# Value tiles of one bank and late mirror products in the first block of an FFT and gated-FFN kernel, with one shared stage-1 table

## The chip, the cores and the metric

One of the eight cores of a Trainium2 chip (trn2). The first rounds of experiments ran on chip 7, those that start with after_again on chip 0 and the last three on chip 7 again, each time with the kernel before in the same rounds. The metric is the device time in microseconds (us) of one execution, as the median of several. The profile gives a second figure, the span from the first to the last instruction, which is 1.7 to 2.1 us shorter; each timed execution lists it. "Product" alone means an elementwise product on VectorE (DVE); ScalarE is ACT, TensorE PE, GpSimd POOL.

## The reference, cut to what matters

```python
def _attn_ref(x):                       # x: (8, 3008, 256), fp32
    X = np.fft.fft(x, axis=1)
    X = np.fft.fft(X, axis=2)
    return X.real.astype(np.float32)

def _moe_ref(x, w_gate, w_val, w_out):  # x: (24064, 256), d_ff 1536
    gate = np.maximum(x @ w_gate, 0.0)
    val = x @ w_val
    return (gate * val @ w_out).astype(np.float32)
```

The kernel does the long transform in two stages (94 times 32 points), folds the transform over 256 into the weights, and uses the mirror symmetry of a real input's transform: from one set of matmuls it gets the gate and value of a frequency ("direct") and, after one more matmul that adds in place, those of the mirrored frequency. A batch has three blocks of 512 columns; a block has 12 steps f (t counts steps over all blocks). The first block (t from 0 to 11) is the only one in which DVE makes both products; later, POOL makes the mirror product and steps go in pairs.

## The kernel before

The value tile of a first-block step takes two banks of PSUM and uses one; there are two such tiles. The mirror matmul (`k == 2`) adds into the bank that the direct product reads.

```python
    psv = ctx.enter_context(tc.tile_pool(name="psv", bufs=2, space=PS))
    # ...
    def early(name):                       # PSUM tiles of the start: value and output tiles in turn
        turn["v"] += 1
        return psv.tile([128, 2, 512], F32, tag="v", name=name)[:, 0, :] if turn["v"] % 2 else spare(name)
    # ...
    def gate(t):                           # two matmuls into a gate bank (of two), then Relu on ACT
        # ...
        nc.scalar.activation(pair(t, "gs")[:, t % 2, ds], G[:, ds], ACTF.Relu)

    def mirror_gate(t):                    # adds into the same bank, after that Relu has read it
        # ...
    # ... the first block:
    for t in range(NF + 1):
        if t:
            mirror_gate(t - 1)
        if t < NF:
            gate(t)
        if t:
            value(t - 1, 2)
            mirror_h(t - 1, 1, nc.vector, pair(t - 1, "V"))
        if t < NF:
            value(t, 0)
            value(t, 1)
            direct_h(t, 1)
            between(t)                     # weight folding, stage 2 of the next blocks: t = 0 to 8 only
```

In the start, the first gate weights arrive by DMA, DVE makes their sum and their difference, and the first fold takes both:

```python
    def pair_w(n, i, eng, parts=(0, 1)):
        lo, hi, up = (wst[i, n, c] for c in range(3))
        if 0 in parts:
            eng.tensor_tensor(up, lo, hi, op=ALU.add)
        if 1 in parts:
            eng.tensor_tensor(lo, lo, hi, op=ALU.subtract)

    def fold_w(n, i, cs, ps=None):
        ps = ps or spare("psw")
        for k, w in ((0, wst[i, n, 2]), (1, wst[i, n, 0])):          # the sum, the difference
            nc.tensor.matmul(ps[64 * k:64 * k + 64, :], lhsT=cd[:, cs, 64 * k:64 * k + 64], rhs=w,
                             start=True, stop=True)
        # ... evictions
```

`cd` is the D table, the cosines and sines with which the fold multiplies the weights: three activations on ACT. The stage-1 table `wn` lives in a pool that closes after the start, so ACT copies half of it to `w1` for the later batches.

Of the kernel before, what the change touches and what calls it, by code (L numbers as in the profile page):

```python
# [11 lines left out]
F32 = mybir.dt.float32  # L12
BF16 = mybir.dt.bfloat16
I32 = mybir.dt.int32
ALU = mybir.AluOpType
ACTF = mybir.ActivationFunctionType
SB = bass.MemoryType.SB
PS = bass.MemoryType.PSUM
# [26 lines left out]
def kernel(ctx: ExitStack, tc, x, w_gate, w_val, w_out, out):  # L45
# [3 lines left out]
    nc = tc.nc  # L49
    B, S, D = x.shape  # L50
    DF = w_gate.shape[1]
    NA, NB = 94, 32
    H = D // 2
    NF = DF // 128
# [7 lines left out]
    tp = ctx.enter_context(tc.tile_pool(name="tp", bufs=2, space=SB))  # L62
    hp = ctx.enter_context(tc.tile_pool(name="hp", bufs=HB, space=SB))
    psg = ctx.enter_context(tc.tile_pool(name="psg", bufs=2, space=PS))
    psv = ctx.enter_context(tc.tile_pool(name="psv", bufs=2, space=PS))
    pso = ctx.enter_context(tc.tile_pool(name="pso", bufs=1, space=PS))
    pqp = ctx.enter_context(tc.tile_pool(name="pqp", bufs=5, space=SB))

    ctx.enter_context(tc.manual_schedule())

# [64 lines left out]
                in_offset=bass.IndirectOffsetOnAxis(ap=ixf[:, k:k + 1], axis=0))  # L135

    turn = {"o": 0, "v": 0}

    def spare(name):

        turn["o"] += 1
        return pso.tile([128, 512], F32, tag=f"o{turn['o'] % 2}", name=name)
# [5 lines left out]
    def early(name):  # L148

        turn["v"] += 1  # L150
        return psv.tile([128, 2, 512], F32, tag="v", name=name)[:, 0, :] if turn["v"] % 2 else spare(name)

    t1t = {}

    def stage1(b, c, evac):

        ps, eo = borrow("ps1"), xt[b]["eo"]
        for i in range(2):
            jj = 2 * c + i
            o = ps[0:96, i * D:(i + 1) * D]  # L160
            if jj:
                nc.tensor.matmul(o, lhsT=w1[:, jj, :], rhs=eo[:, jj, :], start=True, stop=True)  # L162
                continue
            for cs, lo, hi in ((0, 0, H + 1), (1, H + 1, D)):
                for k in range(2):
                    nc.tensor.matmul(ps[0:96, lo:hi], lhsT=wz[:, cs, k, :], rhs=eo[:, k * (J - 1), lo:hi],  # L166
                                     start=(k == 0), stop=(k == 1))
        evacuate(b, c, ps, evac)
# [9 lines left out]
        else:  # L178
            nc.vector.tensor_copy(dst, src)

    psf, tabs = {}, {}

    def ends(r, n):

# [99 lines left out]


    ix = const.tile([96, 2, B], I32, tag="ix")
    w1 = const.tile([NA, 16, 96], BF16, tag="w1")
    wz = const.tile([NA, 3, 2, 96], BF16, tag="wz")
    m2 = const.tile([128, 2, 128], BF16, tag="m2")
    rot = const.tile([128, 128], BF16, tag="rot")  # L290
# [57 lines left out]
    with tc.tile_pool(name="sp", bufs=1, space=SB) as sp:  # L348
        dve, pl = nc.vector, nc.gpsimd

        def residue(t, q, n, eng):

            eng.tensor_scalar(q, t, scalar1=1.0 / n, scalar2=RND, op0=ALU.mult, op1=ALU.add)
            eng.tensor_scalar(q, q, scalar1=-RND, scalar2=float(n), op0=ALU.add, op1=ALU.mult)
            eng.tensor_tensor(t, t, q, op=ALU.subtract)

        def sines(out, r, n, sign):
            nc.scalar.activation(out, r, ACTF.Sin, scale=sign * 2.0 * math.pi / n * (1.0 - 2e-7))

        def cosines(out, a, n):  # L360

            nc.scalar.activation(out, a, ACTF.Sin, scale=-2.0 * math.pi / n, bias=qpi[0:a.shape[0], :])

        def absolute(out, a):
            nc.scalar.activation(out, a, ACTF.Abs)
# [1 line left out]
        def iota(eng, out, pattern, base, mult):  # L367
            eng.iota(out, pattern=pattern, base=base, channel_multiplier=mult, allow_small_or_imprecise_dtypes=True)

        wn = tabs["wn"] = sp.tile([NA, 2, 16, 96], BF16, tag="wn", name="wn")  # L370
        tabs["wzn"] = sp.tile([NA, 2, 96], BF16, tag="wzn", name="wzn")
        tabs["back"] = sp.tile([NA, NB, H], BF16, tag="back", name="back")
        ixf = sp.tile([96, 3], I32, tag="ixf")
# [60 lines left out]
        def bits(shift, mask):  # L434
            ti = sp.tile([128, 1], I32, tag=f"b{shift}{mask}i")
            dve.tensor_scalar(ti[:], pi[:], scalar1=shift, scalar2=mask,
                              op0=ALU.logical_shift_right, op1=ALU.bitwise_and)
            tf = sp.tile([128, 1], F32, tag=f"b{shift}{mask}f")
            dve.tensor_copy(tf[:], ti[:])
            return tf  # L440
# [23 lines left out]
        for k in range(2):  # L464
            sines(free(wz[:], 192 * (k + 1), [97, 2], [2, 48]), both[0], S, 2.0 * k - 1.0)
        nc.scalar.mul(wn[:, 0, 9:16, :], wn[:, 1, 9:16, :], -1.0)
        nc.scalar.copy(w1[:, 1:10, :], wn[:, 1, 1:10, :])
        back(0, 2, "dve")
        dve.tensor_scalar(da[:], dd[:], scalar1=mi[:], scalar2=None, op0=ALU.mult)
        residue(da[:], dq[:], D, dve)  # L470
        jj, sl, up, odd = bits(0, 15), bits(4, 1), bits(5, 3), bits(0, 1)

        ends(24, 8)
# [34 lines left out]
        ends(16, 4)  # L508
        back(16, 4, "dve")
        dve.tensor_scalar(tis[:], tis[:], scalar1=NB - 1, scalar2=None, op0=ALU.bitwise_and)  # L510
        absolute(dq[:], da[:])
        cosines(cd[:, 0, 1:H], dq[:, 1:H], D)
        sines(cd[:, 1, 1:H], da[:, 1:H], D, 1.0)
        group((6, 7, 0), False)
        first_evac(4, "act")
        nc.sync.dma_start(out=seen[:], in_=t1t[0][0:1, 0, 8:10])
# [10 lines left out]
        first_evac(0, "dve")  # L527
        for cs in range(2):
            dve.tensor_tensor(m2[:, cs, :].rearrange("p (u k) -> p u k", u=4), sv[cs][:], ui[:], op=ALU.mult)
        nc.scalar.copy(w1[:, 10:16, :], wn[:, 1, 10:16, :])  # L530

        iota(pl, di[:], [[-32, 4], [-16, 2], [-1, 16]], 0, 1)
        pl.tensor_scalar(s2[:], mi[:], scalar1=1.0, scalar2=-2.0, op0=ALU.min, op1=ALU.mult)
# [43 lines left out]
    op = ctx.enter_context(tc.tile_pool(name="op", bufs=2, space=SB))  # L577

    steps = [(b, blk, f) for b in range(B) for blk in range(NBLK) for f in range(NF)]
    pairs = {}  # L580

    LO, HI = NB // 2, 512 - NB // 2

# [5 lines left out]
    def direct(t):  # L589

        blk = steps[t][1]
        return slice(LO if blk == 0 else 0, HI + 1 if blk == NBLK - 1 else 512)

    def split(t):

        return t >= NF

    def pair(t, name):

        e = pairs.setdefault(t // 2, {})  # L600
        if name == "V" and not split(t):
            name = f"V{t % 2}"
            if name not in e:
                e[name] = psv.tile([128, 2, 512], F32, tag="v", name="V")
            return e[name]
        if name not in e:
            pool, shape, dt = {"h": (hp, [128, 2, 2, 512], BF16), "gs": (gp, [128, 2, 512], F32),
                               "V": (psv, [128, 2, 512], F32), "gm": (ep, [128, 2, 512], F32),
                               "E": (ep, [128, 2, 512], F32)}[name]
            e[name] = pool.tile(shape, dt, tag=name.lower(), name=name)  # L610
        return e[name]
# [3 lines left out]
    def gate(t):  # L615
        b, blk, f = steps[t]
        pq, fs, ds = pqt[b, blk], slice(f * 128, (f + 1) * 128), direct(t)
        G = Gt[t] = psg.tile([128, 512], F32, tag="g", name="G")
        nc.tensor.matmul(G[:, ds], lhsT=wc[0][:, fs], rhs=pq[:, 0, ds], start=True, stop=False)  # L619
        nc.tensor.matmul(G[:, ds], lhsT=ws[0][:, fs], rhs=pq[:, 1, ds], start=False, stop=True)  # L620
        nc.scalar.activation(pair(t, "gs")[:, t % 2, ds], G[:, ds], ACTF.Relu)  # L621
# [8 lines left out]
    def value(t, k):  # L630
        b, blk, f = steps[t]
        cs = mirrored(t) if k == 2 else direct(t)
        w = (wc, ws, wm)[k][1]
        nc.tensor.matmul(pair(t, "V")[:, t % 2, cs], lhsT=w[:, f * 128:(f + 1) * 128],  # L634
                         rhs=pqt[b, blk][:, min(k, 1), cs], start=(k == 0), stop=(k > 0 or split(t)),
                         skip_group_check=(k == 2 or k == 1 and split(t)))

# [6 lines left out]
    def direct_h(t, n):  # L644

        ds, k = direct(t), slice(t % 2, t % 2 + n)
        nc.vector.tensor_tensor(pair(t, "h")[:, k, 0, 0:ds.stop - ds.start], pair(t, "gs")[:, k, ds],  # L647
                                pair(t, "V")[:, k, ds], op=ALU.mult)

    def mirror_h(t, n, eng, val):  # L650

        cols, k = mirrored(t), slice(t % 2, t % 2 + n)
        w = cols.stop - cols.start
        eng.tensor_tensor(free(pair(t, "h")[:], 1024 * (t % 2) + 512 + w - 1, [1024, n], [-1, w]),  # L654
                          pair(t, "gm")[:, k, cols], val[:, k, cols], op=ALU.mult)

    def mirror_value(p):
        t = 2 * p
# [126 lines left out]
    def between(t):  # L785
        for fn in extra.get(t, ()):
            fn()
        pace(t)

    for t in range(NF + 1):  # L790
        if t:
            mirror_gate(t - 1)
        if t < NF:
            gate(t)
        if t:
            value(t - 1, 2)
            mirror_h(t - 1, 1, nc.vector, pair(t - 1, "V"))
        if t < NF:
            value(t, 0)
            value(t, 1)  # L800
            direct_h(t, 1)
            between(t)

    for p in range(NF // 2, n + NF // 2):
        t = 2 * p
        live = p < n
        if NF // 2 < p <= n:
            mirror_gate(t - 1)
        if live:
            value(t, 0)  # L810
            value(t + 1, 0)
            gate(t)
        out_piece(t - NF, 0)
        between(t)
        if NF // 2 < p <= n:
            direct_h(t - 2, 2)
        if live:
            even(t)
            even(t + 1)
        out_piece(t - NF, 1)  # L820
        if live:
            mirror_gate(t)
            gate(t + 1)
        out_piece(t + 1 - NF, 0)
        between(t + 1)
        if NF // 2 < p <= n:
            mirror_value(p - 1)
        if live:
            value(t, 1)
            value(t + 1, 1)  # L830
        out_piece(t + 1 - NF, 1)
# [30 lines left out]
```

## Time and profile before

| | before |
|---|---|
| time, median of the first 3 runs | 624.94 us (624.94 to 625.77) |
| span of the profiled run | 623.9 us |
| PE busy | 612.0 us, 98% of the span |
| start of DVE's sum of the first gate weights | 15.21 us |
| first gate matmul of step 0 | 21.99 us |
| first output matmul (step 12) | 51.81 us |

The prediction below shows the lines of the page and of the views. A row has the start, the duration, engine and source line, operation, what is written from what, shapes, a count of merged rows, and in brackets the idle time before and what ended it.

```profile
15.21 0.69 DVE L321 TENSOR_TENSOR wst<-wst 128x512 f32<-128x512 f32 x1 [0.53 <-DMA wst<-in_moe_w_gate_dram]
15.94 0.69 DVE L323 TENSOR_TENSOR wst<-wst 128x512 f32<-128x512 f32 x1
16.62 1.13 PE L333 MATMUL psw<-wst,cd 128*64 128x512 f32 x4
```

DVE waits for the weights, makes the sum (15.21) and the difference (15.94, ready at 16.63).

### The profile page before, as it was taken

How to read it: one execution, taken by the hardware profiler on the slowest of the kernel's cores; microseconds unless marked ns; L12 is line 12 of the kernel's file. 1: busy time of each engine (PE TensorE's matmuls, PEld its weight loads, DVE VectorE, ACT ScalarE, POOL GpSimd, SP SyncE). 2: the span in 40 equal slices, each digit the busy share in tenths (PEclk: the TensorE clock that was granted, in tenths of full speed). 3: DMA queues.
4: the chain of work that ended last, by engine and by line, in shares of the span. 5: the costliest groups of instructions: out<-in, count | busy, mean ns of one | idle time of the engine just before them, and what ended most of it. 6: DMA issues, size and time to landing. Idle time of an engine off the chain costs nothing.

```text
span 623.9 us, 11929 instructions
## 1 busy us (share of the span) xinstructions
PE 612.0 (98%) x4252; PEld 409.3 (66%) x4284; DVE 536.7 (86%) x652; ACT 445.5 (71%) x857; POOL 520.0 (83%) x447
## 2 busy tenths in 40 slices
PE   8999999999999999999999999999999999999996
PEld 4345666766666666666667666666666666666665
DVE  7677898899889898888988998898988888899991
ACT  7676777777776767767677767767677776766660
POOL 8898898999888898899988998888988965565664
PEclk9999999999999999999999999999999999999998
DMA  8994282525553182613833255531822134112114
GB/s 168 240 169 109 82 219 67 134 65 163 125 136 79 34 234 71 164 36 86 222 100 92 63 162 127 134 82 34 230 72 61 34 85 125 52 34 67 34 35 99
DMA packets 42038, 67.44 MB, mean 108 GB/s; under 512 B 5877, under 2 KB 31774, under 8 KB 39962
## 3 DMA queue, kind: packets, MB, share of 16 engines
q1 hardware_dynamic: 37162, 50.61, 31.4%
q0 software_dynamic: 4656, 15.88, 10.7%
q8 instruction: 33, 0.54, 0.4%
q10 hardware_dynamic: 160, 0.20, 0.1%
q14 instruction: 27, 0.22, 0.1%
HBM read 38.85 MB, written 30.17 MB: 111 GB/s over the span
## 4 chain that ended last, share of the span: by engine, by line
PE 96%; DMA 1%; POOL 1%; issue 1%; DVE 1%; ACT 0%; POOLq 0%; DVEq 0%
PE po L683 40%; PE V L634 19%; PE G L619 10%; PE G L626 10%; PE G L620 10%; PE psw L333 2%; PE ps L162 2%; PE ps L271 2%; DMA lo<-in_x_dram 1%; POOL hi L132 0%; DVE h L647 0%; PE pst L240 0%; PE ps L216 0%; PE ps L166 0%; POOL lo L129 0%
## 5 line engine op out<-in xcount | busy, mean ns | idle before, releaser
L654 POOL TENSOR_TENSOR h<-gm,E 128x992 bf16<-128x992 f32 (+1 forms) x138 | 319.9, 2318 | 83.3 <-DVE E L661 54.4
L683 PE MATMUL po<-wo,h 128*128 128x256 bf16 (+2 forms) x2304 | 328.5, 272 | 0.4
L683 PEld LDWEIGHTS <-h 128*128 128x128 bf16 (+2 forms) x2304 | 231.4, 103 | 105.9
L628 ACT ACTIVATE gm<-G 128x496 f32<-128x496 f32 (+1 forms) x288 | 170.4, 592 | 94.7 <-PE G L626 87.7
L647 DVE TENSOR_TENSOR h<-gs,V 128x1024 bf16<-128x1024 f32 (+3 forms) x150 | 173.8, 1159 | 59.4 <-PE V L634 39.3
L641 DVE SCALAR_TENSOR_TENSOR E<-nb,af,V 128x496 f32<-128x496 bf16 (+1 forms) x276 | 190.2, 731 | 0.4 <-PE G L620 0.4
L621 ACT ACTIVATE gs<-G 128x497 f32<-128x497 f32 (+2 forms) x288 | 169.7, 589 | 25.3 <-PE G L620 25.2
L661 DVE SCALAR_TENSOR_TENSOR E<-E,V 128x992 f32<-128x992 f32 (+1 forms) x138 | 164.6, 1193 | 0.0
L619 PE MATMUL G<-pq,wc 128*128 128x496 bf16 (+2 forms) x287 | 107.6, 375 | 1.2
L620 PE MATMUL G<-pq,ws 128*128 128x497 bf16 (+2 forms) x288 | 108.0, 375 | 0.1
L626 PE MATMUL G<-pq,wm 128*128 128x496 bf16 (+1 forms) x288 | 107.9, 375 | 0.0
L634 PE MATMUL V<-pq,ws 128*128 128x496 bf16 (+2 forms) x280 | 83.7, 374 | 0.0
L634 PE MATMUL V<-pq,wc 128*128 128x496 bf16 (+2 forms) x266 | 80.7, 374 | 0.0
L620 PEld LDWEIGHTS <-ws 128*128 128x128 bf16 x288 | 28.2, 98 | 32.6
L696 ACT COPY os<-po 128x512 f32<-128x512 f32 x63 | 36.9, 586 | 14.3 <-PE po L683 11.7
L634 PEld LDWEIGHTS <-wc 128*128 128x128 bf16 x288 | 28.2, 98 | 20.7 <-issue 2.5
L114 POOL TENSOR_TENSOR eo<-xla 94x256 bf16<-94x256 f32 x56 | 40.5, 729 | 0.6
L619 PEld LDWEIGHTS <-wc 128*128 128x128 bf16 x288 | 28.2, 98 | 18.5 <-DVE pq L278 0.8
L114 POOL TENSOR_TENSOR eo<-xlb 94x256 bf16<-94x256 f32 (+1 forms) x42 | 34.4, 820 | 0.7
L111 POOL TENSOR_TENSOR xla<-xla,xha 94x510 f32<-94x510 f32 x28 | 32.9, 1175 | 2.2
L177 ACT CAST t<-ps 96x512 bf16<-96x512 f32 x56 | 32.7, 584 | 2.3 <-PE ps L162 0.2
L626 PEld LDWEIGHTS <-wm 128*128 128x128 bf16 x288 | 28.1, 98 | 4.4 <-issue 1.6
(142 smaller groups left out, 367.8 us busy)
## 6 DMA issues: line engine op xcount, KB each, us to landing
out_dram<-os SPq DMA_DIRECT2D x124, 128.0 KB
Td<-t SPq DMA_DIRECT2D x7, 768.0 KB
t<-Td SPq DMA_DIRECT2D x7, 768.0 KB
out_dram<-os SPq DMA_DIRECT2D x82, 64.0 KB
xla<-in_x_dram SPq DMA_DIRECT2D x7, 720.0 KB
xlb<-in_x_dram SPq DMA_DIRECT2D x6, 640.0 KB
nb<-Nd SPq DMA_DIRECT2D x23, 128.0 KB
out_dram<-os SPq DMA_DIRECT2D x40, 48.0 KB
```

The source lines that it names most:

```text
L114: yield eng.tensor_tensor(e1[:, :, k:k + H], x1[:, :, 0:H], free(x1, D, [DX, n], [-1, H]), op=op)
L619: nc.tensor.matmul(G[:, ds], lhsT=wc[0][:, fs], rhs=pq[:, 0, ds], start=True, stop=False)
L620: nc.tensor.matmul(G[:, ds], lhsT=ws[0][:, fs], rhs=pq[:, 1, ds], start=False, stop=True)
L621: nc.scalar.activation(pair(t, "gs")[:, t % 2, ds], G[:, ds], ACTF.Relu)
L626: nc.tensor.matmul(G[:, cols], lhsT=wm[0][:, f * 128:(f + 1) * 128], rhs=pqt[b, blk][:, 1, cols], start=False, stop=True, skip_group_check ...
L628: nc.scalar.activation(pair(t, "gm")[:, t % 2, cols], G[:, cols], ACTF.Relu)
L634: nc.tensor.matmul(pair(t, "V")[:, t % 2, cs], lhsT=w[:, f * 128:(f + 1) * 128], rhs=pqt[b, blk][:, min(k, 1), cs], start=(k == 0), stop=( ...
L641: nc.vector.scalar_tensor_tensor(pair(t, "E")[:, t % 2, cols], nbt[b, blk][:, cols], af[:, f:f + 1], pair(t, "V")[:, t % 2, cols], op0=ALU ...
L647: nc.vector.tensor_tensor(pair(t, "h")[:, k, 0, 0:ds.stop - ds.start], pair(t, "gs")[:, k, ds], pair(t, "V")[:, k, ds], op=ALU.mult)
L654: eng.tensor_tensor(free(pair(t, "h")[:], 1024 * (t % 2) + 512 + w - 1, [1024, n], [-1, w]), pair(t, "gm")[:, k, cols], val[:, k, cols], o ...
L661: nc.vector.scalar_tensor_tensor(E[:, :, cols], E[:, :, cols], 2.0, V[:, :, cols], op0=ALU.mult, op1=ALU.subtract)
L683: nc.tensor.matmul(po[0:m, i, :], lhsT=pair(t - f + ff, "h")[:, ff % 2, sg, g * 128:g * 128 + m], rhs=wo[:, ff, :], start=(ff == 0), stop= ...
```

## The change

Its intent: give each value of the first block its own bank, so that the mirror matmul and the mirror product can come one step late, after the direct product of the next step; give the start four tiles where it had two; move the D table ahead on ACT; keep the table `wn` for the whole run and drop the copy, paying for its room with one of the five buffers of pq, the transformed block that the gate and value matmuls read.

```diff
-    psv = ctx.enter_context(tc.tile_pool(name="psv", bufs=2, space=PS))
     pso = ctx.enter_context(tc.tile_pool(name="pso", bufs=1, space=PS))
-    pqp = ctx.enter_context(tc.tile_pool(name="pqp", bufs=5, space=SB))
+    singles = ctx.enter_context(ExitStack())
+    ps1 = singles.enter_context(tc.tile_pool(name="psf", bufs=4, space=PS))
+    pqp = ctx.enter_context(tc.tile_pool(name="pqp", bufs=4, space=SB))
...
-        return psv.tile([128, 2, 512], F32, tag="v", name=name)[:, 0, :] if turn["v"] % 2 else spare(name)
+        return ps1.tile([128, 512], F32, tag="v", name=name) if turn["v"] % 2 else spare(name)
...
-                nc.tensor.matmul(o, lhsT=w1[:, jj, :], rhs=eo[:, jj, :], start=True, stop=True)
+                nc.tensor.matmul(o, lhsT=wn[:, 1, jj, :], rhs=eo[:, jj, :], start=True, stop=True)
...
-        nc.scalar.copy(w1[:, 1:10, :], wn[:, 1, 1:10, :])
...
         residue(da[:], dq[:], D, dve)
+        absolute(dq[:], da[:])
+        cosines(cd[:, 0, 1:H], dq[:, 1:H], D)
+        sines(cd[:, 1, 1:H], da[:, 1:H], D, 1.0)
... (these three lines stood after the eighth input part; a second copy to w1 goes too)
-    for t in range(NF + 1):
+    for t in range(NF):
         if t:
             mirror_gate(t - 1)
-        if t < NF:
-            gate(t)
+        gate(t)
+        value(t, 0)
+        value(t, 1)
+        direct_h(t, 1)
         if t:
-            value(t - 1, 2)
-            mirror_h(t - 1, 1, nc.vector, pair(t - 1, "V"))
... 
+            last_value(t - 1)
+        between(t)
...
+        if p == NF // 2:
+            gate(t)
+            last_value(t - 1)
+            singles.close()
+            psv = ctx.enter_context(tc.tile_pool(name="psv", bufs=2, space=PS))
```

The last lines are the hand-over at step 12: the pool of four small tiles is closed and its banks go to the two-bank tiles of the later blocks.

More of the change, by code (lines that the diff above doesn't have):

```diff
@@ L137 @@
     turn = {"o": 0, "v": 0}
+    tabs = {}
     def spare(name):
@@ L179, in evacuate @@
             nc.vector.tensor_copy(dst, src)
-    psf, tabs = {}, {}
+    psf = {}
     def ends(r, n):
@@ L286 @@
     ix = const.tile([96, 2, B], I32, tag="ix")
-    w1 = const.tile([NA, 16, 96], BF16, tag="w1")
+    wn = tabs["wn"] = const.tile([NA, 2, 16, 96], BF16, tag="wn", name="wn")
     wz = const.tile([NA, 3, 2, 96], BF16, tag="wz")
@@ L368, in iota @@
             eng.iota(out, pattern=pattern, base=base, channel_multiplier=mult, allow_small_or_imprecise_dtypes=True)
-        wn = tabs["wn"] = sp.tile([NA, 2, 16, 96], BF16, tag="wn", name="wn")
         tabs["wzn"] = sp.tile([NA, 2, 96], BF16, tag="wzn", name="wzn")
@@ L510 @@
         dve.tensor_scalar(tis[:], tis[:], scalar1=NB - 1, scalar2=None, op0=ALU.bitwise_and)
-        absolute(dq[:], da[:])
-        cosines(cd[:, 0, 1:H], dq[:, 1:H], D)
-        sines(cd[:, 1, 1:H], da[:, 1:H], D, 1.0)
         group((6, 7, 0), False)
@@ L529 @@
             dve.tensor_tensor(m2[:, cs, :].rearrange("p (u k) -> p u k", u=4), sv[cs][:], ui[:], op=ALU.mult)
-        nc.scalar.copy(w1[:, 10:16, :], wn[:, 1, 10:16, :])
         iota(pl, di[:], [[-32, 4], [-16, 2], [-1, 16]], 0, 1)
@@ L579 @@
     steps = [(b, blk, f) for b in range(B) for blk in range(NBLK) for f in range(NF)]
-    pairs = {}
+    pairs, singly, psv = {}, {}, None
     LO, HI = NB // 2, 512 - NB // 2
@@ L596, in split, with single @@
         return t >= NF
+    def single(t):
+        if t not in singly:
+            singly[t] = ps1.tile([128, 512], F32, tag="v", name="V")
+        return singly[t].unsqueeze(1)
     def pair(t, name):
         e = pairs.setdefault(t // 2, {})
-        if name == "V" and not split(t):
-            name = f"V{t % 2}"
-            if name not in e:
-                e[name] = psv.tile([128, 2, 512], F32, tag="v", name="V")
-            return e[name]
         if name not in e:
@@ L633, in value @@
         w = (wc, ws, wm)[k][1]
-        nc.tensor.matmul(pair(t, "V")[:, t % 2, cs], lhsT=w[:, f * 128:(f + 1) * 128],
+        o = pair(t, "V")[:, t % 2, cs] if split(t) else single(t)[:, 0, cs]
+        nc.tensor.matmul(o, lhsT=w[:, f * 128:(f + 1) * 128],
                          rhs=pqt[b, blk][:, min(k, 1), cs], start=(k == 0), stop=(k > 0 or split(t)),
@@ L646, in direct_h @@
         ds, k = direct(t), slice(t % 2, t % 2 + n)
+        val = pair(t, "V")[:, k, ds] if split(t) else single(t)[:, :, ds]
         nc.vector.tensor_tensor(pair(t, "h")[:, k, 0, 0:ds.stop - ds.start], pair(t, "gs")[:, k, ds],
-                                pair(t, "V")[:, k, ds], op=ALU.mult)
+                                val, op=ALU.mult)
     def mirror_h(t, n, eng, val):
@@ L654, in mirror_h @@
         eng.tensor_tensor(free(pair(t, "h")[:], 1024 * (t % 2) + 512 + w - 1, [1024, n], [-1, w]),
-                          pair(t, "gm")[:, k, cols], val[:, k, cols], op=ALU.mult)
+                          pair(t, "gm")[:, k, cols], val[:, :, cols], op=ALU.mult)
     def mirror_value(p):
@@ L788, in between, with last_value @@
         pace(t)
-    for t in range(NF + 1):
+    def last_value(t):
+        value(t, 2)
+        mirror_h(t, 1, nc.vector, single(t))
+    for t in range(NF):
         if t:
             mirror_gate(t - 1)
-        if t < NF:
-            gate(t)
+        gate(t)
+        value(t, 0)
+        value(t, 1)
+        direct_h(t, 1)
         if t:
-            value(t - 1, 2)
-            mirror_h(t - 1, 1, nc.vector, pair(t - 1, "V"))
-        if t < NF:
-            value(t, 0)
-            value(t, 1)
-            direct_h(t, 1)
-            between(t)
+            last_value(t - 1)
+        between(t)
     for p in range(NF // 2, n + NF // 2):
@@ L806 @@
         live = p < n
-        if NF // 2 < p <= n:
+        if p <= n:
             mirror_gate(t - 1)
+        if p == NF // 2:
[3 more added lines that the diff above has]
+            psv = ctx.enter_context(tc.tile_pool(name="psv", bufs=2, space=PS))
         if live:
@@ L811 @@
             value(t + 1, 0)
-            gate(t)
+            if p > NF // 2:
+                gate(t)
         out_piece(t - NF, 0)
```

## The prediction

> **What bounds the kernel now.** I read the page first (busy shares), then the busy time of each engine in seven stretches, then PE's waits over the whole span, then the order in time where PE is not full.
>
> ```profile
> PE 612.0 (98%) x4252; PEld 409.3 (66%) x4284; DVE 536.7 (86%) x652; ACT 445.5 (71%) x857; POOL 520.0 (83%) x447
> ...
> PE 96%; DMA 1%; POOL 1%; issue 1%; DVE 1%; ACT 0%; POOLq 0%; DVEq 0%
> ```
>
> PE is busy in 98% of the span, and 96% of the chain that ended last is PE. So only holes in PE are worth time. The busy time by stretches (length, then PE, PEld, DVE, ACT, POOL) says where the holes are:
>
> ```profile
> 0.00:16.60 16.60, 13.84 (x92) 8.24 (x93) 12.83 (x54) 12.45 (x28) 12.79 (x34) 1.00 0.76 158
> 16.60:22.00 5.40, 5.40 (x36) 1.79 (x35) 3.77 (x9) 3.92 (x8) 5.16 (x6) 1.00 0.84 255
> 22.00:45.00 23.00, 22.80 (x136) 8.76 (x135) 16.00 (x26) 16.31 (x33) 21.68 (x26) 1.00 1.02 213
> 45.00:51.80 6.80, 5.35 (x23) 2.12 (x22) 4.76 (x9) 3.77 (x8) 6.41 (x12) 1.00 0.51 108
> 51.80:100.00 48.20, 48.04 (x344) 33.14 (x346) 41.34 (x47) 36.72 (x70) 42.17 (x38) 1.00 0.48 126
> 100.00:560.00 460.00, 458.74 (x3222) 314.23 (x3244) 410.36 (x456) 338.83 (x649) 394.79 (x313) 1.00 0.40 105
> ```
>
> After 51.8 us PE is full. Holes are in the first 16.6 us (tables and first input) and from 45.0 to 51.8, the last four f steps of the first block, where no weight folding is left to fill PE. PE's waits over the whole span, all before 52 us:
>
> ```profile
> PE V L634 <- DVE h L647: 1.4, 3, 0.8
> PE psk L398 <- DVE wk L392: 1.3, 1, 1.3
> PE ps L216 <- DVE hi L190: 0.9, 1, 0.9
> PE ps L216 <- ACT t L230: 0.4, 1, 0.4
> PE psw L333 <- DVE wm L327: 0.2, 1, 0.2
> ```
>
> The change can touch the first and the fourth. The first in order of time (step 10 and the hand-over to step 12; G is the gate, V the value, wm the mirror weights):
>
> ```profile
> 48.22 0.37 PE L620 MATMUL G<-pq,ws 128*128 128x496 bf16 x1
> 48.24 0.66 DVE L647 TENSOR_TENSOR h<-gs,V 128x496 bf16<-128x496 f32 x1
> 48.69 0.58 ACT L621 ACTIVATE gs<-G 128x496 f32<-128x496 f32 x1
> 48.96 0.37 PE L634 MATMUL V<-pq,wm 128*128 128x496 bf16 x1 [0.36 <-DVE h L647]
> 49.44 0.67 DVE L654 TENSOR_TENSOR h<-gm,V 128x496 bf16<-128x496 f32 x1 [0.53 <-PE V L634]
> 50.02 0.67 DVE L647 TENSOR_TENSOR h<-gs,V 128x496 bf16<-128x496 f32 x1
> 50.74 0.37 PE L634 MATMUL V<-pq,wm 128*128 128x496 bf16 x1 [0.79 <-DVE h L647]
> ```
>
> The value's mirror matmul adds in place into the bank that the direct product h is still reading, so PE stands until that DVE product ends (48.24 + 0.66 = 48.90, PE at 48.96). DVE takes the mirror product of the step before first. The loop is V mirror, mirror product, direct product, V mirror: 48.96 to 50.74, 1.78 us a step, against six matmuls of 0.21 = 1.25 us.
>
> **What the Trainium skill says.** "TensorE: Matmul & The Clock Gate", section "Step-by-step: what each phase is for", puts the back-to-back gap of matmuls at N / 2.4 GHz plus about 2.5 ns: 209 ns at 496 columns. The trace agrees: 49.17, 49.38, 49.58. Its section "Architectural detail: the array is 16× 32×32, not 1× 128×128" calls ACT and DVE strict FIFO; agreed, the direct product waits behind the mirror product above. "PSUM — Partial Sum Buffer", section "Terms", gives eight banks of 2 KiB a partition, 512 fp32: the value tiles of before take two banks and use one, so four one-bank tiles fit the same room. "ScalarE: Activation LUTs", section "What ACT_TABLE_LOAD costs", gives 186 ns + 0.833 ns an element, 599 ns at 496, with overlap of about 93 ns; here 0.58, every 0.48.
>
> **The change part by part.**
>
> **1. First block.** Built orders show, per step t: G mirror(t-1), G(t) two, V(t) two, and only then V mirror(t-1); on DVE the direct product of t before the mirror product of t-1. Steps 0 to 8 have folding matmuls between them and PE holes of 0.2 us in 23, so nothing moves there. For steps 9 on I lay out the new order with durations from this trace (matmul issue 0.21, to result 0.37, 0.1 on to ACT; Relu 0.58, a second one 0.48 later; product 0.66, a second one 0.59 later; 0.05 from an end to PE), in the clock of before, from the second G matmul of step 9 at 45.05.
> - V(9) 45.26 and 45.47, V mirror(8) 45.68 without a wait (its direct product ended 45.34).
> - G mirror(9) must wait for the Relu of G(9), which ran 45.52 to 46.10: 46.15, as before. This read of the gate's bank takes the place of the wait removed. Then 46.36, 46.57, 46.78, 46.98, V mirror(9) 47.19.
> - Relu of G(10): 47.03 to 47.61, G mirror(10) 47.66. So a step is 1.51 us (0.37 + 0.1 + 0.58 + 0.05 + two matmuls), not 1.78 and not 1.25. Then G(11) 47.87 and 48.08, V(11), V mirror(10) 48.70.
> - Relu of G(11) to 49.12, G mirror(11) 49.17, G(12) 49.38 and 49.59. The direct product of 11 runs 49.16 to 49.82, V mirror(11) 49.89.
> - **The hand-over.** Four small value tiles give way to two large ones. In the built program the first value matmul of step 12 waits for the DVE count that the mirror product of step 11 raises, that is, for all small tiles. That product needs V mirror(11), 50.26, and follows the mirror product of 10 (49.75): 50.34 to 51.01. V(12) at 51.07 and 51.29, the first output matmul at 51.50.
> Before, that output matmul stood at 51.81. Gain 0.31 us. PE's holes from 45.05 on were 0.14 + 0.13 + 0.41 + 0.53 + 0.95 = 2.16 us (start to start, less 0.21); they become 3 x 0.26 + 0.09 + 0.97 = 1.84.
>
> **2. Four one-bank tiles in the start, and the D table sooner.** Two waits go.
>
> ```profile
> 11.77 0.10 PEld L216 LDWEIGHTS <-lo 94*128 94x128 bf16 x1 [0.24 <-issue]
> 11.93 0.49 PE L216 MATMUL ps<-wn,back 94*128 94x192 bf16 x4
> 13.98 0.29 ACT L358 ACTIVATE cd<-da 128x127 f32<-128x127 f32 x1
> 14.18 0.87 ACT L230 CAST t<-ps 128x384 bf16<-128x384 f32 x2
> 14.71 0.24 PE L216 MATMUL ps<-wz,lo 94*128 94x192 bf16 x1 [0.43 <-ACT t L230]
> ```
>
> At 11.77 PE waited 0.25 us for a value tile (the third taken, of two); with four it doesn't. Four warming matmuls follow, then the group that needs hi's DVE copy (12.91), so that group comes only 0.16 sooner: its first tile is done at 13.63, not 13.79. Its eviction stood on ACT behind the three D table activations until 14.18; now they run near 8.2 in ACT's idle time before 9.80, in the place of the table copy removed there, and the eviction can start at 13.70. The matmul at 14.71 comes 0.53 later: 14.23, a gain of 0.48. Then the first fold would start at 16.14 in place of 16.62, but its second half needs the DVE difference of the weights that ends at 16.63, so it starts at 16.69 in place of 17.12. Gain kept 0.43, less 0.01 on DVE's later evictions: 0.42.
>
> **3. One table, no copy.** ACT loses two copies (0.89 and 0.67). At 8.20 it idled afterwards, and at 17.14 the next eviction waits for PE anyway: 0. The room comes from pq, five buffers to four: the third block of the next batch is written from step 35 of a batch and reuses a block last read at about step 24. 0.
>
> Sum: 0.31 + 0.42 = 0.73 us. 624.94 - 0.73 = 624.2.
>
> **The rivals.**
> - **A: all that wait was PE's loss.** If nothing took its place, the 2.16 us go and with part 2 the time is 622.4. For: the waits view puts 1.4 us on the direct product alone. Against: the gate's Relu is read by PE within the same step, and the hand-over waits for the last product.
> - **B: the new hand-over costs as much as it saves**, or the start is held by the weights' transfer (landing at 15.2) all the same. Then 624.6 to 625.0. For: V mirror(11) and two DVE products in a row end only 0.1 to 0.2 us before the old point; ACT or DVE 0.1 us later each step undoes the gain.
> - **C: the moved D table delays the first evictions, or four pq buffers stall stage 2.** Then 625.5 or more. Against: ACT idles 0.71 us before 9.80, after a copy longer than the table; PE has no listed wait after 52 us.
>
> **Range and chances.** Three runs of before lie in 0.83 us, more than the gain. 2% is 12.5 us, more than all PE holes of the span. I take 624.2, range 623.3 to 625.1; faster 0.01, same 0.985, slower 0.005.
>
> **What would show it.** Right: PE's first fold near 16.2, first output matmul near 51.1 (51.81 before), G mirror of steps 10 and 11 about 1.5 us apart, the first value matmul of step 12 waiting about 1 us on DVE's mirror product. Wrong: that last wait absent or under 0.3 us (rival A), a first output matmul after 51.6 (B), or PE waits after 52 us (C).

## The result, and the profile after

| | before | after |
|---|---|---|
| time, median of 6 runs each | 624.98 us (624.79 to 626.04) | 624.93 us (624.80 to 625.44) |
| ratio | | 0.9996, interval 0.9983 to 1.0009 |
| span of the profiled run | 623.9 us | 623.1 us |
| start of DVE's sum of the first gate weights | 15.21 | 14.82 |
| first gate matmul | 21.99 | 21.56 |
| first output matmul | 51.81 | 51.10 |

A ratio compares the runs of two kernels in the same rounds, so it is not quite the ratio of the medians quoted. The time lies in the range that was forecast. The profiled spans seem to bear the 0.73 us out (0.8 us less), and the first output matmul came at 51.10 where the forecast said "near 51.1". That is a trap, as the experiments show: half of it is an accident of when the weights landed in the two profiled runs.

The time and the span do not move together here. In the 18 runs of the kernel before in the first two sets of rounds the time is 1.72 to 1.82 us longer than the span; in the 11 runs of the kernel after (six here, five in after_again) it is 1.77 to 2.06 us longer. By the means, the span fell by 0.32 us (623.37 to 623.05) and the time by 0.16 (on chip 0 alone by 0.23 and 0.11). So half of what the span gains doesn't reach the time. It is lost outside the first and last instruction, where the profile shows nothing; no run says why.

The page of the kernel after, busy times and the chain that ended last:

```profile
PE 612.1 (98%) x4252; PEld 409.3 (66%) x4284; DVE 536.5 (86%) x652; ACT 444.4 (71%) x855; POOL 520.2 (83%) x447
...
PE 96%; DMA 1%; issue 1%; ACT 1%; DVE 1%; POOL 0%; POOLq 0%
```

PE still bounds everything. PE's busy time in the two early stretches that had holes (length, then busy time of PE, PEld, DVE, ACT, POOL, each with its count):

```profile
0.00:16.60 16.60, 14.41 (x95) 8.44 (x97) 13.30 (x55) 12.51 (x28) 13.08 (x34) 1.00 0.78 168
...
45.00:51.80 6.80, 5.61 (x28) 2.59 (x27) 5.36 (x10) 3.87 (x8) 6.41 (x12) 1.00 0.65 134
```

PE's waits: the three on the direct product (1.4 us) and the one on an eviction in the start (0.4 us) are gone, and two are new.

```profile
PE V L635 <- DVE h L656: 0.8, 1, 0.8
PE ps L218 <- DMA lo<-in_x_dram: 0.2, 1, 0.2
```

The second is a wait for the first input, which landed sooner or later from run to run. The first in order of time. G is the gate bank, `gs` and `gm` its Relu before and after the mirror matmul, `wm` the mirror weights:

```profile
47.66 0.37 PE L620 MATMUL G<-pq,ws 128*128 128x496 bf16 x1
48.13 0.58 ACT L621 ACTIVATE gs<-G 128x496 f32<-128x496 f32 x1
48.76 0.37 PE L626 MATMUL G<-pq,wm 128*128 128x496 bf16 x1
...
49.33 1.28 DVE L656 TENSOR_TENSOR h<-gm,V 128x496 bf16<-128x496 f32 x2
49.47 0.37 PE L635 MATMUL V<-pq,wm 128*128 128x496 bf16 x1
50.67 0.59 PE L635 MATMUL V<-pq,wc 128*128 128x512 bf16 x2 [0.83 <-DVE h L656]
```

Two things are to be seen. The gate mirror at 48.76 stands until the Relu that began at 48.13 has read the bank (48.71): this read took the place of the one removed, and a step is 1.51 us. And the first value matmul of step 12 stands 0.83 us, until the second of the two mirror products (49.33 to 50.61) has ended, because the closed pool is handed on only when all its tiles have been read. The start, in order of time:

```profile
14.82 0.69 DVE L323 TENSOR_TENSOR wst<-wst 128x512 f32<-128x512 f32 x1 [0.43 <-DMA wst<-in_moe_w_gate_dram]
15.54 0.69 DVE L325 TENSOR_TENSOR wst<-wst 128x512 f32<-128x512 f32 x1
15.56 1.80 PE L335 MATMUL psw<-wst,cd 128*64 128x512 f32 x4
16.29 0.19 PEld L335 LDWEIGHTS psw<-wst,cd 128*64 128x64 f32 x2 [0.53 <-DVE wst L325]
```

The fold starts 1.06 us sooner than before (15.56, not 16.62). Of this, 0.60 us was there at the first product already (9.75, not 10.35), as the input landed sooner in this run (the two other profiles with the old start have 9.57 and 9.65); 0.46 us came in between, close to the 0.48 forecast. Then the fold's second half stands until DVE's difference is there (15.54 + 0.69 = 16.23), and the fold takes 1.80 us in place of 1.13. What the start had gained was given back there.

### The profile page after: what moved, and what is told of

The parts are those of the page before. It is cut to its first block, busy times and chain, and to the rows that moved or that the text cites. A ratio compares the mean times of both kernels' runs of the same rounds, so it can differ in the third digit from the quotient of the medians. Undisturbed runs are those within 1.5% of the kernel's fastest.

```text
span 623.1 us, 11916 instructions
## 1 busy us (share of the span) xinstructions
PE 612.1 (98%) x4252; PEld 409.3 (66%) x4284; DVE 536.5 (86%) x652; ACT 444.4 (71%) x855; POOL 520.2 (83%) x447
## 3 DMA queue, kind: packets, MB, share of 16 engines
q1 hardware_dynamic: 37162, 50.61, 31.2%
## 4 chain that ended last, share of the span: by engine, by line
PE 96%; DMA 1%; issue 1%; ACT 1%; DVE 1%; POOL 0%; POOLq 0%
PE po L685 40%; PE V L635 19%; PE G L619 10%; PE G L626 10%; PE G L620 10%; PE psw L335 2%; PE ps L164 2%; PE ps L273 2%; DMA hi<-in_x_dram,ixf 1%; PE ps L218 1%; PE pst L242 0%; PE ps L168 0%; ACT gs L621 0%; ACT gm L628 0%; DVE h L656 0%
```

## The experiments

The question was where the other half of the gain is. **Theory W**: the start is bound by the landing of the weights plus DVE's two instructions, before the change as after, so the start's part of the change is worth next to nothing, and only the first block's 0.3 us is left. **Rival P**, the prediction: the start is worth 0.42 us. A second question is whether the waits that took the old one's place are what the lines above suggest.

Stages read from the profile of each run. S is the start of DVE's sum of the gate weights, G0 the first gate matmul, O the first output matmul; each column is a difference of starts in us. From O to the end it is 571.8 to 572.2 us in every kernel. The times come from different rounds, in which the median of the kernel before was 624.98, 625.00 or 625.08.

| kernel | S | S to G0 | G0 to O | span | median time |
|---|---|---|---|---|---|
| before | 15.21 | 6.78 | 29.82 | 623.9 | 624.98 |
| after | 14.82 | 6.74 | 29.54 | 623.1 | 624.93 |
| after_again | 14.37 | 6.77 | 29.54 | 622.5 | 624.95 |
| start_only | 14.59 | 6.74 | 29.84 | 623.1 | 624.93 |
| loop_only | 14.82 | 6.95 | 29.54 | 623.2 | 625.23 |
| before_w | 14.56 | 6.75 | 29.84 | 623.0 | 625.05 |
| after_w | 14.94 | 6.74 | 29.54 | 623.1 | 625.06 |
| early_four | 14.77 | 6.74 | 30.40 | 624.1 | 625.38 |
| late_two | 15.20 | 6.75 | 30.92 | 624.8 | 626.36 |
| gate_late | 15.01 | 6.75 | 30.72 | 624.3 | 625.94 |
| two_handovers | 15.05 | 6.75 | 28.54 | 622.2 | 623.80 |
| third_gate | 14.34 | 6.82 | 27.84 | 621.0 | 622.96 |
| third_gate_w | 14.49 | 6.75 | 27.84 | 621.1 | 623.21 |

The table shows the trap at once: S differs by up to 0.87 us from run to run with no regard to the kernel, and G0 follows it (in third_gate 0.08 us later, as the sum itself took 0.77 and not 0.69 us). The kernel before had happened to be profiled with weights that landed late (15.21). In its nine runs of the first round of experiments its span was 623.1 to 624.0, mean 623.44; 623.9 is the slow end of that.

The traces show the tie to the weights more closely. In 12 of the 13 profiles, old start or new, the first fold ends 1.12 or 1.13 us after DVE's difference is there (before: 16.63 to 17.75; before_w: 15.98 to 17.11; after: 16.23 to 17.36). Only in loop_only is it 1.25 us.

### start_only: the start of the change alone

```diff
 # the kernel before, with
+    singles = ctx.enter_context(ExitStack())
+    ps1 = singles.enter_context(tc.tile_pool(name="psf", bufs=4, space=PS))
+        return ps1.tile([128, 512], F32, tag="v", name=name) if turn["v"] % 2 else spare(name)
+        # the three lines of the D table after residue(da[:], dq[:], D, dve)
+    singles.close()                        # ahead of the first block
+    psv = ctx.enter_context(tc.tile_pool(name="psv", bufs=2, space=PS))
     for t in range(NF + 1):
```

> The start of the change alone (four one-bank tiles until the first block, D table sooner), first block as before. Theory W (weights bind): the second half of the first fold matmul waits for the DVE difference of the gate weights in both kernels, so from the start of that sum on DVE (15.21 before, 14.82 after) to the first gate matmul it stays 6.75 us (6.78 before, 6.74 after), and the time is that of before within 0.1 us. Rival P (the prediction's part 2): the start is worth 0.42 us; with the weights landing at 15.2 the first gate matmul comes at 21.57, so 6.36 us from the sum, and the time falls by 0.4 us. First gate matmul to first output matmul: 29.8 us in both, as before.

Measured: 624.93 us (5 runs), the kernel before 625.00 (9 runs), ratio 0.9997 (0.9983 to 1.0010). S to G0 is 6.74 us. Its order of time at the fold:

```profile
14.59 0.69 DVE L322 TENSOR_TENSOR wst<-wst 128x512 f32<-128x512 f32 x1 [0.51 <-DMA wst<-in_moe_w_gate_dram]
15.32 0.69 DVE L324 TENSOR_TENSOR wst<-wst 128x512 f32<-128x512 f32 x1
15.52 1.62 PE L334 MATMUL psw<-wst,cd 128*64 128x512 f32 x4
```

The first-stage products ended early, as the change intends, and the fold waited within itself for the difference (16.01): 1.62 us long. Theory W's number came out, rival P's 6.36 did not. The times alone could not have told them apart, as the interval is wider than 0.4 us.

### loop_only: the first block of the change alone

```diff
 # the kernel after (one table, no copy, four pq buffers), with the tiles and the D table of the old start
-    ps1 = singles.enter_context(tc.tile_pool(name="psf", bufs=4, space=PS))
+    ps1 = singles.enter_context(tc.tile_pool(name="psf", bufs=2, space=PS))
-        return ps1.tile([128, 512], F32, tag="v", name=name) if turn["v"] % 2 else spare(name)
+        return ps1.tile([128, 2, 512], F32, tag="v", name=name)[:, 0, :] if turn["v"] % 2 else spare(name)
+        # the D table back in its old place
+    singles.close(); singles = ctx.enter_context(ExitStack())
+    ps1 = singles.enter_context(tc.tile_pool(name="psb", bufs=4, space=PS))
     for t in range(NF):
```

> The first block of the change alone (four one-bank value tiles, late mirrors, hand-over at step 12); the start with two two-bank tiles and the D table late, as before. Theory W: all of the change's gain is here: first gate matmul to first output matmul 29.5 us (29.82 before, 29.54 after), time 0.3 us under before, as the whole change. Rival P: the same 29.5 us here, but the whole change is 0.4 us faster than this run.

Measured: G0 to O 29.54 us, as forecast by both and as in the change. The time is 625.23 us, ratio 1.0000 (0.9987 to 1.0014); the 0.3 us do not show in it, and the interval is too wide to deny them. Rival P's second number isn't denied by the times either: the whole change is 0.3 us faster than this run by the medians, in other rounds. In this one profile S to G0 is 6.95 us:

```profile
15.55 0.69 DVE L325 TENSOR_TENSOR wst<-wst 128x512 f32<-128x512 f32 x1
16.41 1.08 PE L335 MATMUL psw<-wst,cd 128*64 128x512 f32 x4
```

The difference was there at 16.24, but the old start's products held the fold back to 16.41; the old start was late by 0.2 us. So in the three profiles with the old start its delay is 0, 0 and 0.2 us, by which of the two, products or weights, comes last in a run. The mean spans agree: start_only (623.24) is 0.20 us under before (623.44, same chip), and the change (623.03 in its own six runs) is 0.25 us under loop_only (623.28). Each of these differences is within the scatter of the runs. The start's part is thus worth between 0 and about 0.2 us, not 0.42.

### after_again, before_w, after_w: weights issued sooner

The changed kernel once more; and both kernels with the four weight transfers issued ahead of four small POOL instructions.

```diff
+        load_w(0, pl)
         pl.tensor_scalar(perm[:], dd[:], scalar1=mi[:], scalar2=None, op0=ALU.is_equal)
         iota(pl, ui[:], [[1, 4], [0, NB]], 0, 0)
         iota(pl, kbi[:, 0, :], [[1, NB]], NB // 2, 0)
         iota(pl, kbi[:, 1:4, :], [[0, 3], [1, NB]], 0, 0)
-        load_w(0, pl)
```

> The changed kernel once more, on one chip with the three that follow. Span as before in its own rounds, 622.8 to 623.4; first gate matmul about 6.7 to 6.8 us after the start of the gate weights' sum on DVE (theory W), whenever the weights land.

> The kernel before with the transfers of the first gate and value weights issued ahead of five small Pool instructions (about 1 us sooner). Theory W: in the kernel before the first-stage products end (16.5) just as the weights are ready (16.63), so weights that land sooner help little: the first fold still starts at 16.3 to 16.6, first gate matmul 21.7 to 21.9, time that of before within 0.2 us. Rival: the weights alone bound the start of before too; then the first gate matmul comes 0.5 us sooner or more, near 21.3.

> The changed kernel with the same sooner weights. Theory W: here the products end at 15.5 and wait for the weights, so now the start's part of the change shows: both halves of the first fold from 15.5 to 16.6, first gate matmul 20.9 to 21.1 (21.56 in the change), time 0.4 to 0.6 us under the change, and 0.8 us or more under before_w. Rival: the next thing in the start (value weights' pair on Pool, DVE's evictions) is as late; then the first gate matmul stays at 21.4 to 21.6 and the time that of the change.

Measured: after_again 624.95 us, before on the same chip 625.08, ratio 0.9999 (0.9985 to 1.0013); spans 622.5 to 623.7, mean 623.06 against 623.29. S to G0 6.77, as expected. before_w 625.05 and after_w 625.06 us: no change in either. The edit missed its aim. The transfers were issued 1.1 us sooner (8.33 and 8.44, not 9.45 and 9.59), but DVE's sum began at 14.56 and 14.94, within the spread of the other runs. So in these runs the landing does not follow the issue. The mean DMA share from 8 to 15 us is 1.04 in the kernel before and 1.01 in after_w, at 248 and 247 GB/s: the DMA engines are full in that time. It is likely, though not shown by these runs, that the weights just wait behind the first input, which is issued before them. The two forecasts of what sooner weights would bring were therefore not tested. What the pair adds is two more profiles with S to G0 at 6.75 and 6.74, one of them with the old start.

### early_four and late_two: which half of the first-block change does the work

```diff
 # early_four: the kernel after, mirrors where they stood
         gate(t)
+        if t:
+            last_value(t - 1)
         value(t, 0)
         value(t, 1)
         direct_h(t, 1)
-        if t:
-            last_value(t - 1)
 # late_two: the kernel after, two two-bank tiles in the first block
+    ps1 = singles.enter_context(tc.tile_pool(name="psb", bufs=2, space=PS))
-            singly[t] = ps1.tile([128, 512], F32, tag="v", name="V")
+            singly[t] = ps1.tile([128, 2, 512], F32, tag="v", name="V")[:, 0, :]
```

> The change with its four one-bank value tiles, but the mirrors where they were before (value mirror of t-1 ahead of the values of t). Theory: the wait was for the direct product that reads the same bank, not for a free tile, so four tiles alone change nothing: steps 9 to 11 stay 1.78 us, and the hand-over that waits for all small tiles now only costs: first gate matmul to first output matmul 30.4 us (29.82 before), time 0.3 to 0.5 us over before. Rival (tiles were short): steps of 1.5 us, 29.5 us.

> The change with late mirrors, but two value tiles in the first block as before. Theory: the value of t then needs the tile of t-2, whose mirror product now runs only after the direct product of t-1: a step is 0.37 + 0.05 + two products of 0.59 and 0.67 + 0.05 + one matmul 0.21, 1.94 us, more than the 1.78 before; first gate matmul to first output matmul 30.1 us or more, time 0.3 us or more over before. Rival (only the order matters): steps of 1.51 us, 29.5 us.

Measured: early_four 625.38 us, ratio 1.0002 (0.9986 to 1.0017), G0 to O 30.40 as forecast; the last step before the hand-over (second gate matmul to second gate matmul) is 1.79 us, and the hand-over costs its 0.8 us on top. late_two 626.36 us, ratio 1.0016 (1.0000 to 1.0031), steps of 2.00 and 1.99 us (forecast 1.94), G0 to O 30.92. Its wait, in order of time:

```profile
47.12 0.66 DVE L656 TENSOR_TENSOR h<-gm,V 128x496 bf16<-128x496 f32 x1
...
47.83 0.37 PE L635 MATMUL V<-pq,wc 128*128 128x496 bf16 x1 [0.58 <-DVE h L656]
```

The value of a step waits for the mirror product that frees its tile. Neither half gains alone: more tiles without the late order do nothing for the steps, and the late order without more tiles makes the stage longer than before (30.92, not 29.82 us). Only both make 1.51 us.

### two_handovers: the wait at step 12 taken away

Two pools of two banks in place of one of four. The first closes at step 12, when its tiles (steps 8 and 9) have been read; the second at step 14. (The start takes its tiles from both pools in turn; S to G0 stayed at 6.75 us.)

```diff
+    halves = [ctx.enter_context(ExitStack()) for _ in range(2)]
+    ps1 = [None, None]
+    for i in (1, 0):
+        ps1[i] = halves[i].enter_context(tc.tile_pool(name=f"psf{i}", bufs=2, space=PS, side=("left", "right")[i]))
...
-            singly[t] = ps1.tile([128, 512], F32, tag="v", name="V")
+            singly[t] = ps1[t // 2 % 2].tile([128, 512], F32, tag="v", name="V")
...
+        if p < NF // 2 + 2:
+            i = p % 2
+            halves[i].close()
+            psv[i] = ctx.enter_context(tc.tile_pool(name=f"psv{i}", bufs=1, space=PS, side=("left", "right")[i]))
```

> The change with its hand-over at step 12 split: two pools of two banks, the first of which is free when the mirror product of step 9 has been read. If the wait of 0.83 us (1.03 us start to start less 0.21) at the first value matmul of step 12 is a plain loss, it goes: first gate matmul to first output matmul 28.6 us (29.54 in the change), time about 0.9 us under the change. Rival: the two mirror products and the sums of step 12 stand in the same DVE queue, so the wait only moves to a later matmul of steps 12 and 13 and comes back: time that of the change within 0.2 us, and PE waits for DVE between 51 and 55 us.

Measured: 623.80 us (623.75 to 624.23), before 625.00, ratio 0.9977 (0.9964 to 0.9991). G0 to O 28.54 us, 1.00 less than the change.

```profile
49.70 0.37 PE L638 MATMUL V<-pq,wm 128*128 128x496 bf16 x1
...
49.91 0.59 PE L638 MATMUL V<-pq,wc 128*128 128x512 bf16 x2
...
50.34 0.60 PE L688 MATMUL po<-wo,h 128*128 128x256 bf16 x4
```

The value matmuls of step 12 follow the last mirror matmul by one matmul, and PE has no wait for DVE between 51 and 55 us. The wait was a plain loss; the rival falls.

### third_gate, gate_late: the loop through the gate's Relu

```diff
     for t in range(NF):
-        if t:
+        if 0 < t < 9:
             mirror_gate(t - 1)
         gate(t)
+        if t >= 9:
+            mirror_gate(t - 1)
 # third_gate, on top of two_handovers; gate_late, on the change, has the order alone
-        G = Gt[t] = psg.tile([128, 512], F32, tag="g", name="G")
+        G = Gt[t] = spare("G") if t == 10 else psg.tile([128, 512], F32, tag="g", name="G")
```

(In both, the gate mirror of step 11 likewise follows the gate matmuls of step 12.)

> two_handovers, and from step 9 on the gate mirror stands behind the next gate matmuls, with a third gate bank (step 10 in an idle output bank), so that no matmul reads a bank straight after its Relu. If the step of 1.51 us in the change is the loop gate matmul, Relu, gate mirror (0.37 + 0.1 + 0.58 + 0.05 + two matmuls), steps 9 to 11 fall to 1.25 us, the six matmuls: first gate matmul to first output matmul 27.9 us, time 0.7 us under two_handovers. Rival: DVE (two products, 1.18 us a step, in order) or ACT binds before: steps of 1.4 us and more, gain under 0.3 us.

> third_gate's order (gate mirror behind the next gate matmuls from step 9 on) with only two gate banks and the change's hand-over. Theory: the next gate matmul then waits for the Relu of the mirror in the bank it takes: 0.21 + 0.37, first Relu ahead of it on ACT, 1.53 after the gate matmul, so steps of 1.79 us, against 1.51 in the change and 1.25 expected and to be read in third_gate; first gate matmul to first output matmul 30.2 us. Rival (the order alone did it in third_gate): 1.3 us a step, 28.9 us.

Measured: third_gate 622.96 us (622.88 to 623.49), ratio 0.9966 (0.9952 to 0.9979), G0 to O 27.84 us. Its second gate matmuls of steps 10 and 11:

```profile
45.27 0.37 PE L623 MATMUL G<-pq,ws 128*128 128x496 bf16 x1
46.53 0.37 PE L623 MATMUL G<-pq,ws 128*128 128x496 bf16 x1
```

A step is 1.26 us, the six matmuls. With the same order and two gate banks (gate_late) it is 1.73 us (forecast 1.79), since the next gate matmul stands for the Relu of the mirror:

```profile
47.86 0.37 PE L619 MATMUL G<-pq,wc 128*128 128x496 bf16 x1 [0.31 <-ACT gm L628]
```

gate_late took 625.94 us, ratio 1.0010 (0.9994 to 1.0025); its G0 to O is 30.72 where 30.2 was forecast, because its hand-over waits 1.4 us and not the 0.8 us that the forecast took over from the change. So the order needs the third bank, and the 1.51 us of the change was the loop through the Relu.

### third_gate_w

> third_gate with the same sooner weights, as the best of all. If the gains add: the 622.96 of third_gate less the same 0.4 to 0.6 us, 622.4 to 622.6. If not, 622.9.

Measured: 623.21 us (622.95 to 623.57), ratio 0.9972 (0.9958 to 0.9985). No gain on top: S is 14.49, where third_gate without the sooner issue had 14.34. The best kernel is third_gate, some 2 us under both kernels.

## Why the prediction was right or wrong

In the range (623.3 to 625.1) and right on "same". Neither says much: all of PE's holes together are under 2%, so each of the rivals would have given "same" too, and the range takes in all of rival B's. The central value was 0.7 us too low: 624.2 forecast, 624.93 measured, so of a gain of 0.73 us hardly anything shows in the time. One term of the sum was wrong (part 2, by 0.2 to 0.4 us), and about 0.16 us was lost outside the span, which the prediction didn't count and no run explains. The rest is within the scatter. By its own steps:

- **What bounds the kernel**: right. From the first output matmul to the end it is 572 us in every kernel tried; everything happens before 53 us.
- **Part 1, the steps**: right, and near exact. Gate mirror matmuls stand at 1.51 to 1.52 us from each other (45.73, 47.25, 48.76); "not 1.78 and not 1.25" holds, and gate_late and third_gate show that it is the Relu's read of the gate bank.
- **Part 1, the hand-over**: right. A wait of 0.83 us on the last mirror product (0.97 by the forecast's count, start to start less 0.21; measured 50.67 less 49.47 less 0.21 = 0.99). G0 to O fell by 0.28 us, forecast 0.31.
- **Part 2, the start**: the step that failed is "its second half needs the DVE difference of the weights that ends at 16.63, so it starts at 16.69 in place of 17.12". It already started at about 16.68 before: the two halves of the fold go into different column halves of the array and run side by side. The second half alone takes 1.07 us (16.29 to 17.36 in the kernel after), both together 1.08 (loop_only), so the fold that starts at 16.62 and ends at 17.75 had its second half on the way 0.06 us after the first. I had set them one behind the other and put the second half's start about half a fold too late. With that corrected the gain of 0.42 is 0 to 0.2 us: the fold's end was set by the weights before, or by both at once, and is set by the weights after. The 12 profiles with 1.12 or 1.13 us from the difference to the fold's end show it, start_only among them (S to G0 6.74 against 6.78). Two waits did go from PE in the kernel after, as forecast (in late_two and gate_late, with the same new start, an eviction wait of 0.4 and 0.2 us is back), and the products were 0.46 us quicker, as forecast; the time was then spent at the next wait, which the waits view of the kernel before could not show, as PE reached it just when it was over.
- **A reading**: rival C is answered with "a copy longer than the table"; the copy takes 0.89 us and the table 0.93 (13.34 to 14.27). The table still fitted: in the kernel after it ended at 9.13, and ACT's next eviction came at 9.20.
- **Part 3**: no cost was seen in the span: no listed PE wait after 52 us, and O to the end is unchanged. The single table and the four pq buffers were not run by themselves.
- **The signs named**: "first fold near 16.2" was wrong as a sign (15.56, and it told nothing, as 0.60 us of it was the input's landing), "first output matmul near 51.1" came out (51.10) for a wrong reason, 0.39 us of it being the weights' earlier landing in that run.
- **The rivals**: A falls; B is half right, by its clause that the start is held by the weights' transfer all the same, and its 624.6 to 625.0 holds the measured time; C falls, as no PE wait appeared after 52 us.

## What to carry to other kernels

When a wait on one reader of a bank is removed, list the other readers of the same step and of the tile's release: here the Relu of the gate and the closing of a pool gave back about 1.9 of 2.16 us (the stage shrank from 29.82 to 29.54 us), and nearly all of it could be had back with one more gate bank, a later gate mirror and a split pool (27.84 us). An engine that arrives at a wait just as it ends shows no wait in the profile; before counting a gain, ask for every input of the next instruction when it was ready. And where a transfer's landing varies by more than the effect, compare intervals from that landing, not absolute times of two profiles.

## What the Trainium skill lacked or had wrong

- No page tells that banks handed from one tile pool to another can wait for all of the old pool's tiles: 0.83 us of PE here, gone (623.80 us) with two pools.
- "TensorEngine Tiling (Array Packing)", section "Key Properties", says that different tiles of the array run matmuls in parallel; the runs agree and add a number: the fold's two column halves take 1.08 us when both inputs are there at the start, and 1.62 to 1.80 us when the second comes 0.5 to 0.7 us late. The page doesn't warn that a late half loses the overlap.
- "DMA: Bandwidth & Descriptors" lacks a figure for how far a landing spreads from run to run: here DVE's sum, which starts on the landing, began between 14.34 and 15.21 us over 13 profiles, and transfers issued 1.1 us sooner did not land sooner, with a mean DMA share of 1.0 from 8 to 15 us.
- "ScalarE: Activation LUTs", section "What ACT_TABLE_LOAD costs": 599 ns at 496 elements stands against a mean of 584 ns for the 96 gate Relus of that size in the kernel before, a small difference.
